# Six short GpSimd instructions in place of one long one: scaling the blocks of q tile by tile

## The chip, the cores and the metric

The kernel runs on one core of a Trainium2 chip. The metric is the device time of one execution in microseconds (us); lower is better. The engines of the core go by the profile's names: PE (TensorE matmul), PEld (TensorE weight load), DVE (VectorE), ACT (ScalarE), POOL (GpSimd), and SP (SyncE, which issues most DMAs). Each works through its own list of instructions in program order; semaphores tie the lists together.

## The reference

Windowed attention feeds a mixture of experts with one expert per token, and that feeds a two-layer network with a squared ReLU. Cut to what matters here:

```python
def _attn_ref(q, k, v):                      # q, k, v: (4, 8, 576, 64)
    scale = 1.0 / np.sqrt(D)                 # 0.125
    scores = scale * np.matmul(q, k.transpose(0, 1, 3, 2))
    ...                                      # heads 0-3: window 32; heads 4-7: window 32, dilation 4
    scores = np.where(masks[None, :, :, :], scores, -1000000000.0)
    scores = scores - np.max(scores, axis=-1, keepdims=True)
    attn = np.exp(scores)
    attn = attn / (np.sum(attn, axis=-1, keepdims=True) + 1e-09)
    return np.matmul(attn, v)

def _moe_ref(x, modality_id, w_gate, modality_bias, w1, w2):   # x: (2304, 512), 8 experts
    logits = x @ w_gate + modality_bias[modality_id]
    e_idx = np.argmax(logits, axis=1)
    ...                                      # gate_w: softmax weight of the chosen expert
    out[mask] = gate_w[mask, None] * (np.maximum(x[mask] @ w1[e], 0.0) @ w2[e])

def _moe2_ref(x, w_in, w_out):               # d_ff 2048
    h = np.maximum(x @ w_in, 0.0)
    return h * h @ w_out
```

## The kernel before, in words

**Attention.** There are 8 groups (4 batches, each with its plain and its dilated heads) of 6 tiles of 96 queries, so 48 units, handled one per round of a loop in `schedule`. For a unit, `A` writes the mask and the scores into a PSUM bank (the matmuls of L318 and L321, which read `q` and `kd`) and DVE takes the negated row maximum `nm` (L324). `C` is the exponential on ACT (`p`, L333). `D` transposes `p` on PE (L343) and copies it out on ACT (`pt`). `F` multiplies with `v` (L357) and DVE normalizes out of PSUM: `rs` (L360), its reciprocal `rc` (L363), the product `x` (L366). `H` transposes `x` on PE (L396), ACT copies the high part `xth` (L399), and DVE forms the low part `xtl` (L400) from the PSUM bank and `xth`. The steps of one round belong to different units: L396 in one round works on `x` of an earlier one, and it needs a bank from which `xtl` of the unit before has been read.

**Where q is scaled.** In the first round of a group, `A` calls `load` for the next group: SP issues the DMA of the whole block of q (128 partitions, 6 tiles, 2 x 96 columns, so 1152 numbers a partition) and of k, and GpSimd multiplies q by 0.125 in place (L299). The very first group is loaded in two halves; DVE scales the first half, GpSimd the second. So GpSimd has eight such instructions, one of 576 and seven of 1152 numbers a partition.

**What else DVE does.** One-time preparation (`setup`, up to L265) runs in round 3. Once a batch is through attention, `route` (L425 on, once a batch) and `select` (L529 on) work out which token goes to which expert. They are chains of very small DVE instructions on SBUF tiles; `schedule` deals them out between the attention steps of later rounds, a few at a time, in the fixed order of the program. So DVE's list alternates between attention steps, most of which read PSUM, and these small steps, most of which read and write SBUF only.

**Afterwards.** The experts' matmuls (class `Moe`) start between the last units and go on alone; the last stage (`Ffn`) decodes its weights with DVE, ACT and GpSimd (L864 to L880; `da` is the decoded tile, `raw` the loaded one), squares on GpSimd or DVE (`fsq`, L950), and multiplies (L940, L985). PE works through all of it in one fixed list.

Of the kernel before, what the change touches and what calls it, by code (L numbers as in the profile page):

```python
# [18 lines left out]
ALU = mybir.AluOpType  # L19
# [173 lines left out]
class Attention:  # L193
# [82 lines left out]
    def load(self, g, what):  # L276
        nc, ins = self.g.nc, self.g.ins
        if g >= 2 * B:
            return
        b, kind = divmod(g, 2)  # L280
        if "q" in what:
            self.qt[g] = self.qp.tile([128, NTL, 2, QT], F32, tag="q", name="q")
        if "v" in what:
            self.vt[g] = self.vp.tile([128, NTL, 260], F32, tag="v", name="v")
        plan = START if g == 0 else tuple((w, 0, NTL) for w in what)
        for w, t0, t1 in plan:
            if w == "i":
                nc.sync.dma_start(out=self.g.ident, in_=ins["c_ident"])
                continue
            if w == "m":  # L290
                nc.sync.dma_start(out=self.cmask, in_=ins["c_masks"])
                continue
            if w == "v":
                nc.sync.dma_start(out=self.vt[g][:, t0:t1], in_=ins["v"][b, kind, :, t0:t1])
                continue
            c0, c1 = t0 * QT, t1 * QT
            q = self.qt[g][:, t0:t1]
            nc.sync.dma_start(out=q, in_=ins["q"][b, kind, :, t0:t1])
            (nc.vector if g == 0 and t0 == 0 else nc.gpsimd).tensor_scalar(out=q, in0=q, scalar1=0.125, scalar2=None, op0=ALU.mult)  # L299
            for hb in range(2):  # L300
                nc.sync.dma_start(out=self.kd[g % 2][64 * hb:64 * hb + 64, :, hb, 32 + c0:32 + c1],
                                  in_=ins["k"][b, kind, 64 * hb:64 * hb + 64, :, c0:c1])
# [776 lines left out]
```

## Time and profile before

| | before |
|---|---|
| time, median of 3 runs (lowest, highest) | 828.16 us (826.91, 830.04) |
| the profiled execution: its time, its span | 828.4 us, 826.6 us |
| busy share of the span: PE, PEld | 96%, 82% |
| busy share of the span: DVE, ACT, POOL | 52%, 39%, 21% |
| mean granted clock of TensorE | 0.985 |

The span is the time from the first to the last instruction on the core; the 1.8 us between it and the time are outside the instructions. A busy share is a mean over stages with different limits, so POOL's 21% says nothing yet on whether one of its instructions holds somebody up. Rows of a timeline give the start, the duration, the engine, the line of the kernel, the operation, and the tile written and read; a bracket at the end is the idle time of that engine just ahead of the row, and what ended it. The granted clock is a share of TensorE's full speed.

### The profile page before, as it was taken

To read this page: it belongs to the slowest core of one execution; us is meant where nothing else is said; L and a number is where in the kernel's file an instruction comes from. 1 tells how busy PE (TensorE), PEld (TensorE's weight loads), DVE (VectorE), ACT (ScalarE), POOL (GpSimd) and SP (SyncE) were. 2 spreads that over 40 slices of the span, in tenths; PEclk is the share of its full clock that TensorE was granted. 3 is DMA by queue.
4 is the path that set the end of the run, shared out by engine and by line. 5 is a ranking of instruction groups with operands and counts; after the bars stand their busy time and mean duration, and the time that the engine had idled before them with its cause. 6 is when DMAs were issued, how large, how long until landed. Compare 5 with 4: busy or idle time off the path is not lost.

```text
span 826.6 us, 12554 instructions
## 1 busy us (share of the span) xinstructions
PE 790.4 (96%) x4273; PEld 675.3 (82%) x4273; DVE 428.9 (52%) x1124; ACT 325.2 (39%) x779; POOL 169.5 (21%) x197
## 2 busy tenths in 40 slices
PE   8999887899999999999898899999999999999996
PEld 5878776678888888888776789989989989998995
DVE  5787879743347777552399952242233234224222
ACT  3767656522244555552344532232232232223221
POOL 3135432014213333201155530010001001001001
PEclk9999988999999999999999999999999999999999
DMA  7666456020324444531245500010001001001000
GB/s 211 148 180 179 125 149 230 21 70 27 90 77 128 119 138 128 192 141 54 83 123 148 147 38 27 1 43 9 26 14 39 26 2 51 0 1 39 1 1 38
DMA packets 44810, 67.40 MB, mean 82 GB/s; under 512 B 6816, under 2 KB 28672, under 8 KB 44224
## 3 DMA queue, kind: packets, MB, share of 16 engines
q1 hardware_dynamic: 38720, 50.75, 21.2%
q0 software_dynamic: 3280, 10.76, 4.3%
q10 hardware_dynamic: 2736, 4.99, 1.6%
q8 instruction: 35, 0.57, 0.3%
q14 instruction: 39, 0.32, 0.1%
HBM read 129.65 MB, written 14.44 MB: 174 GB/s over the span
## 4 chain that ended last, share of the span: by engine, by line
issue 40%; DVE 5%; PE 2%; POOL 2%; DMA 1%; ACT 1%; POOLq 0%; ACTq 0%; DVEq 0%; SPq 0%
POOL out L990 1%; DMA raw<-in_wo 1%; DVE da L875 1%; PE bk L940 1%; DVE da L869 1%; DVE da L864 1%; DVE fhl L959 1%; PE bk L753 1%; DVE da L872 1%; PE bk L985 1%; POOL wol L880 0%; ACT dm L862 0%; ACT woh L879 0%; DVE yl L927 0%; DVE fout L989 0%
## 5 line engine op out<-in xcount | busy, mean ns | idle before, releaser
L950 DVE TENSOR_TENSOR fsq<-fr 128x384 f32<-128x384 f32 x84 | 46.9, 559 | 173.7 <-ACT fr L948 173.7
L940 PE MATMUL bk<-yh,wih 128*128 128x384 f32 x384 | 130.5, 340 | 3.3 <-ACTq L822 1.6
L940 PE MATMUL bk<-yl,wih 128*128 128x384 f32 x384 | 130.1, 339 | 1.3 <-DVE yl L927 1.3
L940 PE MATMUL bk<-yh,wil 128*128 128x384 f32 x384 | 129.9, 338 | 0.0
L948 ACT ACTIVATE fr<-bk 128x384 f32<-128x384 f32 x96 | 46.9, 488 | 188.0 <-PE bk L940 187.3
L985 PE MATMUL bk<-wol,fhh 128*128 128x512 f32 x288 | 113.5, 394 | 3.8 <-POOL wol L880 3.7
L985 PE MATMUL bk<-woh,fhh 128*128 128x512 f32 x288 | 115.0, 399 | 2.1 <-ACT woh L879 2.1
L985 PE MATMUL bk<-woh,fhl 128*128 128x512 f32 x288 | 113.3, 393 | 0.0
L990 POOL DMA_INDIRECT out<-fout,fidx x18 | 18.1, 1006 | 323.3 <-DVE fout L989 320.5
L940 PEld LDWEIGHTS bk<-yh,wih 128*128 128x128 f32 x384 | 72.5, 189 | 8.3 <-ACT yh L926 2.3
L959 DVE TENSOR_TENSOR fhl<-fsq,fhh 128x384 fp32r<-128x384 f32 x96 | 55.5, 578 | 45.0 <-ACT fhh L958 44.7
L940 PEld LDWEIGHTS bk<-yl,wih 128*128 128x128 f32 x384 | 72.4, 189 | 5.8 <-DVE yl L927 2.6
L940 PEld LDWEIGHTS bk<-yh,wil 128*128 128x128 f32 x384 | 72.6, 189 | 0.0
L958 ACT ACTIVATE fhh<-fsq 128x384 fp32r<-128x384 f32 x96 | 50.3, 524 | 50.2 <-DVE fsq L950 48.7
L985 PEld LDWEIGHTS bk<-wol,fhh 128*128 128x128 f32 x288 | 54.2, 188 | 14.4 <-POOL wol L880 6.0
L985 PEld LDWEIGHTS bk<-woh,fhl 128*128 128x128 f32 x288 | 54.2, 188 | 13.1 <-DVE fhl L959 0.4
L723 PE MATMUL bk<-w1h,xh 128*128 128x512 f32 x152 | 63.4, 417 | 0.8 <-DVE htl L739 0.8
L985 PEld LDWEIGHTS bk<-woh,fhh 128*128 128x128 f32 x288 | 54.2, 188 | 11.7 <-ACT woh L879 3.8
L333 ACT ACTIVATE p<-bk,nm 96x128 f32<-96x128 f32 x192 | 53.9, 363 | 19.6 <-DVE nm L324 11.1
L753 PE MATMUL bk<-w2h,hth 128*128 128x512 f32 x152 | 61.0, 401 | 0.0
L723 PE MATMUL bk<-w1l,xh 128*128 128x512 f32 x152 | 60.9, 400 | 0.0
L723 PE MATMUL bk<-w1h,xl 128*128 128x512 f32 x152 | 60.8, 400 | 0.0
(173 smaller groups left out, 1399.8 us busy)
## 6 DMA issues: line engine op xcount, KB each, us to landing
st<-in_w SPq DMA_DIRECT2D x41, 2048.0 KB
raw<-in_wi SPq DMA_DIRECT2D x32, 256.0 KB
raw<-in_wo SPq DMA_DIRECT2D x32, 256.0 KB
v<-in_v SPq DMA_DIRECT2D x7, 780.0 KB
q<-in_q SPq DMA_DIRECT2D x7, 576.0 KB
kd<-in_k SPq DMA_DIRECT2D x14, 288.0 KB
xd<-x SPq DMA_DIRECT2D x40, 96.0 KB
yb<-y ACTq DMA_DIRECT2D x13, 256.5 KB
```

The source lines that it names most:

```text
L333: self.g.nc.scalar.activation(out=p[:, h, :], in_=ps[:, h, :], func=AF.Exp, bias=nm[:, h:h + 1], scale=1.0)
L723: nc.tensor.matmul(ps, a[:, c, :], w[:, c, sl], start=k == 0, stop=k == 11)
L753: nc.tensor.matmul(ps, a[:, c, :], w[:, c, :], start=k == 0, stop=k == 23)
L864: nc.vector.tensor_scalar(out=a, in0=raws[new][:, :, 1], scalar1=3, scalar2=0x3FFFFFF8, op0=ALU.logical_shift_left, op1=ALU.bitwise_and)
L869: nc.vector.scalar_tensor_tensor(out=a, in0=raws.pop(old)[:, :, 0], scalar=29, in1=a, op0=ALU.logical_shift_right, op1=ALU.bitwise_or)
L940: nc.tensor.matmul(ps, w[:, c, f * 128:(f + 1) * 128], a[:, c, :], start=k == 0, stop=k == 11)
L948: nc.scalar.activation(out=r, in_=ps, func=AF.Relu)
L950: (nc.gpsimd if blk == 0 and f > 3 else nc.vector).tensor_tensor(out=s, in0=r, in1=r, op=ALU.mult)
L958: nc.scalar.activation(out=hh, in_=s, func=AF.Copy)
L959: nc.vector.tensor_tensor(out=hl, in0=s, in1=hh.bitcast(F32), op=ALU.subtract)
L985: nc.tensor.matmul(acc[t], a[:, sl], w[:, f, :], start=f == 0 and j == 0, stop=f == NF - 1 and j == 2)
L990: dma = nc.gpsimd.indirect_dma_start(out=out, out_offset=bass.IndirectOffsetOnAxis(ap=self.idx[:, i:i + 1].bitcast(U32), axis=0), in_=o, i ...
```

## The change

Where GpSimd scales a block of q, the loop now issues one instruction per tile of 192 numbers a partition: three for the second half of the first group and six for each of the other seven groups, 45 in place of 8. What DVE scales, the DMAs and all tiles stay as they are. The lines behind the edit move down by five (L321 is L326 and so on).

```diff
             q = self.qt[g][:, t0:t1]
             nc.sync.dma_start(out=q, in_=ins["q"][b, kind, :, t0:t1])
-            (nc.vector if g == 0 and t0 == 0 else nc.gpsimd).tensor_scalar(out=q, in0=q, scalar1=0.125, scalar2=None, op0=ALU.mult)
+            if g == 0 and t0 == 0:
+                nc.vector.tensor_scalar(out=q, in0=q, scalar1=0.125, scalar2=None, op0=ALU.mult)
+            else:
+                for t in range(t0, t1):
+                    q = self.qt[g][:, t]
+                    nc.gpsimd.tensor_scalar(out=q, in0=q, scalar1=0.125, scalar2=None, op0=ALU.mult)
             for hb in range(2):
```

On GpSimd's list, the start of the program before (the half block, the first whole block, three small fills of `setup`, the next block; the brackets are the semaphores that a row waits for, DMAHW those of DMAs):

```order
L299 ISA
L299 TENSOR_SCALAR q<-q 128x576 [waits DMAHW6_49,Pool_49]
L299 TENSOR_SCALAR q<-q 128x1152 [waits DMAHW0_49]
L247 MEMSET reset 96x48
L248 MEMSET reset 96x8 [waits Pool_49]
L249 MEMSET tbl 128x144
L299 TENSOR_SCALAR q<-q 128x1152 [waits DMAHW7_49,DVE_49,PE_49]
```

The same place now:

```order
L304 ISA
L304 TENSOR_SCALAR q<-q 128x192 [waits DMAHW6_49,Pool_49]
L304 TENSOR_SCALAR q<-q 128x192 x2
L304 TENSOR_SCALAR q<-q 128x192 [waits DMAHW0_49]
L304 TENSOR_SCALAR q<-q 128x192 x5
L247 MEMSET reset 96x48
L248 MEMSET reset 96x8 [waits Pool_49]
L249 MEMSET tbl 128x144
L304 TENSOR_SCALAR q<-q 128x192 [waits DMAHW7_49,DVE_49,PE_49]
```

Each long row has become one short row that waits for the DMA, and two or five more that wait for nothing; what stands around them is in the same order as before.

On PE's list, one round of attention in the second group before:

```order
L357 MATMUL bk_70<-v,pt 96x65 x4
L318 LDWEIGHTS mask
L318 MATMUL bk_67<-mask 96x512
L321 MATMUL bk_67<-kd_140,q 96x256 x2
L396 MATMUL bk_73<-ident,x 128x96 [waits DVE_49]
L396 MATMUL bk_73<-ident,x 128x96
```

The same round now:

```order
L362 MATMUL bk_70<-v,pt 96x65 x4
L323 LDWEIGHTS mask
L323 MATMUL bk_67<-mask 96x512
L326 MATMUL bk_67<-kd_140,q 96x256 [waits Pool_49]
L326 MATMUL bk_67<-kd_140,q 96x256
L401 MATMUL bk_73<-ident,x 128x96 [waits DVE_49]
L401 MATMUL bk_73<-ident,x 128x96
```

Every unit's scores now wait for the scaling of their own tile, where only the first unit of a block waited before; no row has changed its place. DVE's, ACT's and SP's lists hold the same rows in the same order.

## Rows read from the trace of the kernel before

**Rows 1.** Timeline, 28.5 to 34 us: a block of q beside attention alone.

```profile
29.11 3.13 POOL L299 TENSOR_SCALAR q<-q 128x1152 f32<-128x1152 f32 x1 [10.42 <-DVE rs L360]
...
30.52 0.34 DVE L400 TENSOR_TENSOR xtl<-bk,xth 128x192 fp32r<-128x192 f32 x1
```

**Rows 2.** Timeline, 14.5 to 20 us: the first place.

```profile
15.17 3.13 POOL L299 TENSOR_SCALAR q<-q 128x1152 f32<-128x1152 f32 x1 [3.48 <-DMA q<-in_q]
15.21 3.06 DVE L265 TENSOR_TENSOR bias<-bias,btmp 96x192 f32<-96x192 f32 x1
...
18.19 0.15 DVE L360 TENSOR_SCALAR rs<-bk 96x4 f32<-96x4 f32 x1
...
19.05 0.39 PE L396 MATMUL bk<-ident,x 96*128 96x96 f32 x2 [2.07 <-DVE x L366]
```

**Rows 3.** Timelines, 57.5 to 66 us: the second place, all engines, then DVE.

```profile
58.12 3.18 POOL L299 TENSOR_SCALAR q<-q 128x1152 f32<-128x1152 f32 x1 [9.51 <-DMA q<-in_q]
...
58.39 2.93 DVE L486 COPY carry<-rcum 96x8 f32<-96x8 f32 x1
...
61.52 0.38 PE L396 MATMUL bk<-ident,x 96*128 96x96 f32 x2 [1.88 <-DVE xtl L400]
...
63.59 0.35 DVE L400 TENSOR_TENSOR xtl<-bk,xth 128x192 fp32r<-128x192 f32 x1
```

**Rows 4.** Timeline, 90 to 96 us: the third place.

```profile
90.64 2.96 DVE L483 TENSOR_TENSOR_SCAN rcum<-reset,rtin 96x48 f32<-96x48 f32 x1
...
94.23 0.39 PE L396 MATMUL bk<-ident,x 96*128 96x96 f32 x2 [2.08 <-DVE xtl L400]
```

**Rows 5.** Timeline, 109.5 to 124 us: the fourth place.

```profile
110.21 3.03 DVE L542 TENSOR_SCALAR scj<-sci 1x8 int32<-1x8 int32 x1
...
115.49 0.58 PE L396 MATMUL bk<-ident,x 96*128 96x96 f32 x2 [2.30 <-DVE xtl L400]
```

**Rows 6.** Windows, PE alone: length, busy (instructions), granted clock, DMA share, GB/s.

```profile
61.50:65.50 4.00, 3.96 (x36) 1.00 0.42 67
94.00:99.00 5.00, 4.77 (x30) 0.66 0.43 101
115.00:122.50 7.50, 7.01 (x33) 0.54 0.62 163
```

**Rows 7.** Groups of POOL instructions by shape.

```profile
L299 POOL TENSOR_SCALAR q<-q 128x1152 f32<-128x1152 f32 x7 | 21.9, 3135 | 56.8 <-DMA q<-in_q 21.0 <-PE bk L357 13.3 <-PE bk L343 12.2
...
L299 POOL TENSOR_SCALAR q<-q 128x576 f32<-128x576 f32 x1 | 1.7, 1677 | 6.8 <-DMA q<-in_q 6.8
```

**Rows 8.** Timeline, 415 to 434 us: two POOL instructions back to back, and DVE.

```profile
418.68 0.74 POOL L880 TENSOR_TENSOR wol<-da,woh 128x256 fp32r<-128x256 f32 x1 [1.20 <-ACT woh L879]
418.71 0.99 DVE L875 SCALAR_TENSOR_TENSOR da<-dm,da 128x256 f32<-128x256 f32 x1
419.38 1.01 POOL L950 TENSOR_TENSOR fsq<-fr 128x384 f32<-128x384 f32 x1
419.62 0.91 DVE L864 TENSOR_SCALAR da<-raw 128x256 int32<-128x256 int32 x1
```

**Rows 9.** Timeline of PE, 0 to 60 us: the mask matmuls of three units.

```profile
15.74 0.38 PE L318 MATMUL bk<-mask 96*96 96x512 bf16 x1
...
26.39 0.38 PE L318 MATMUL bk<-mask 96*96 96x512 bf16 x1
...
28.62 0.38 PE L318 MATMUL bk<-mask 96*96 96x512 bf16 x1
```

**Rows 10.** Waits of PE: engine, line, for whom; us in total, times, longest.

```profile
PE bk L321 <- POOL q L299: 0.2, 1, 0.2
```

**Rows 11.** Timeline, 248 to 252 us: three POOL and DVE rows of the decoding.

```profile
249.16 0.99 POOL L702 DMA_INDIRECT gx<-xd,sc  x1 [0.51 <-POOL sc L701]
...
249.75 1.47 DVE L872 SCALAR_TENSOR_TENSOR da<-raw,da 128x256 int32<-128x256 int32 x1
250.18 0.75 POOL L880 TENSOR_TENSOR wil<-da,wih 128x256 fp32r<-128x256 f32 x1
```

## The prediction

> **What bounds the kernel now.** I first looked at where the edited line lies: all blocks of q are scaled in the first 114 us, in the attention stage. There I read the timeline of all engines around each of the eight GpSimd instructions, to see which other engine changes its pace while one runs. In four of them nobody does. The block from 29.11 to 32.24 [rows 1] is typical: DVE's `xtl`, which reads one PSUM and one SBUF tile, takes its ordinary 0.34 us in the middle of it, and a round of attention lasts 2.23 us (two mask matmuls in a row start at 26.39 and 28.62, [rows 9]), just as without a block. So the busy time of GpSimd itself is not on the path.
>
> In the other four DVE stands still until the GpSimd instruction is over. At 15.21 the last instruction of `setup`, a sum of two SBUF tiles, takes 3.06 us and ends at 18.27, when the scaling ends at 18.30 [rows 2]. At 58.39 a copy of 8 numbers a partition takes 2.93 us and ends at 61.32, the scaling at 61.30 [rows 3]. The scan at 90.64 takes 2.96 us [rows 4], a shift of 8 integers on one partition at 110.21 takes 3.03 us [rows 5]. All four read and write SBUF only. The sizes of these instructions have nothing to do with their times; the end of the GpSimd instruction has.
>
> That reaches the path, since DVE's list mixes these small steps with attention steps. Behind each of them stands an `x` or an `xtl`, and PE's L396 waits for it: 2.07, 1.88, 2.08 and 2.30 us of idle PE [rows 2 to 5], 8.3 us together. There is a second loss: in the five microseconds from 94 us PE has a mean granted clock of 0.66, in the 7.5 from 115 us of 0.54, that is mostly the lower of its levels (1.2 in place of 2.4 GHz), while behind the idle of 1.88 us the clock stayed at 1.00 [rows 6]. In these two windows PE is busy nearly all the time, so its pace sets the rounds.
>
> **The change part by part.** *The short instruction.* The two sizes that ran, 576 and 1152 numbers, took 1677 and 3135 ns [rows 7]: 2.53 ns a number and 0.22 us fixed. One of 192 numbers should take 0.71 us, six of them 4.2 us, so GpSimd works 1.1 us longer for a block, 8 us in all. Nobody waits for that by itself: in the first whole block tile 0 is scaled at 15.9 us and first used after 18 us, and a further tile is wanted only each 2.23 us. PE's 37 added waits find their tile done; I cost them at nothing. If each cost what the separate wait instructions of GpSimd's queue last at most, below 0.05 us, that would be under 2 us, but the other waits on PE's list are of this kind and show no such gap.
>
> *The half block.* PE waited 0.2 us for it [rows 10]. Its first tile is now done a microsecond earlier. k may land no earlier than that, so I take a gain of 0.2, between 0 and 0.3.
>
> *What DVE waits now.* What the trace must tell is whether DVE gets its turn between two GpSimd instructions that stand back to back. In the decoding there is such a pair [rows 8]: L880 ends at 419.42, L950 has begun at 419.38. DVE's L875, which reads two SBUF tiles and started at 418.71, ends at 419.70, well inside L950, which runs to 420.39: it got in at the border. The next DVE instruction, L864, started at 419.62 and then had to wait nearly to the end of L950 (420.53). So they take turns: each GpSimd instruction holds up at most one DVE instruction of this kind, for a little less than its own length. The page SBUF — State Buffer of the Trainium skill (section Who interferes with whom) names the cause: DVE and GpSimd share one port pair under an exclusive lock for a whole instruction, so the loser blocks fully. The first two places bear this out to 0.03 us.
>
> *The first place.* Only one SBUF-only instruction is left in DVE's list there. It gets in at about 15.8 in place of 17.9 us, and the attention steps behind it read PSUM and run freely. PE then has no idle time: its wait for `x` began at 16.98 (19.05 less 2.07), and `x`, which followed 0.86 us behind the start of `rs` at 18.19, is now there by 16.8. From the mask matmul at 15.74 to the one at 26.39 are 10.65 us for three rounds, where three of 2.23 us are 6.7 [rows 9]: 3.9 us lost, idle time, lower clock and late ACT together. I take back 3.7, between 2.1 (idle PE alone) and 3.9.
>
> *The second place.* Here six SBUF-only steps of `route` (L486, L489, L491, L493, L499, L502) follow one another, with `xtl`, `rs`, `rc` and `x` in between. Each meets another of the six short instructions. The copy ended 0.02 us behind the scaling [rows 3] though it needs some 0.17 us itself, so an instruction of 0.71 holds DVE for about 0.55. Going through the list with that, I get waits of about 0.3, 0.55, 0.3, 0.5, 0.25 and 0.4 us: 2.3 us in place of nearly all of 2.93. DVE would reach the second `xtl`, now at 63.59 [rows 3], perhaps 0.1 us earlier. Gain 0.1; the bounds are -1.0 and +1.9 (all of the idle PE).
>
> *The third place.* The same chain from the scan on gives 2.6 us of waits, so DVE gains nearly nothing. But PE's 2.08 us of idle time are split in two of about a microsecond, since the first `xtl` comes early and the second late. Each is shorter than the 1.88 us behind which the clock stayed up, so I expect the full clock: 4.77 us of busy time at 0.66 are 3.15 us at 1.00 [rows 6], a gain of 1.6. Bounds: 0 (clock falls all the same) and 3.7 (with the idle time).
>
> *The fourth place.* In `select` all small steps are SBUF-only, but with attention steps between them; I get waits of 0.45, 0.4, 0.35, 0.1 and 0.5 us, and `nm` and `xtl` 0.7 us earlier. PE's idle time falls from 2.30 to 1.6 us. If the clock stays up, 7.01 us at 0.54 shrink to 3.8 [rows 6], but DVE's chain has to run as well, so of these 3.2 us I count 1.0. Gain 1.7, between 0.7 and 5.5 (2.30 and 3.2).
>
> *The sum*: 0.2 + 3.7 + 0.1 + 1.6 + 1.7 = 7.3 us. What follows is one fixed order on PE, whose loads and weights are issued by the same lists, so I let all of it pass to the end. The profiled execution took 828.4 us, 0.2 over the median of the runs shown: 828.4 - 7.3 = 821.1, say **821.0 us**.
>
> **The rivals.** *(A) The lock isn't given up between the six.* Then DVE waits through the whole block: 4.0 us (six of 0.71, with the small overlaps that back-to-back instructions show) in place of 3.13, in four places, +3.6 us: **832.0**. It decides if DVE misses the first border. For it: DVE's L872 at 249.75 took 1.47 us, past the end of L702 at 250.15 and nearly to that of L880 at 250.93 [rows 11]. Against it: rows 8, where both are element-wise work as here. The GPSIMD Engine Reference of the Trainium skill (section 2.1, Instruction dispatch) says that a core of GpSimd starts the next instruction as soon as its own share is done; by that rule neighbours could overlap and leave no border. In rows 8 the trace doesn't agree; rows 11 would fit.
>
> *(B) Turns cost as much as the long wait.* In the last three places the chains are dense, and PE's clock falls as before: 0.2 + 3.7 + 0.1 + 0 + 0.7 = 4.7, **823.7**. For it: the six waits in a row. Against it: shorter single idles of PE.
>
> *(C) DVE wins most borders.* If GpSimd is slow to come back behind a DVE instruction, several small steps pass at once, and the idle and the low clock go everywhere: 0.2 + 3.9 + 1.9 + 3.7 + 5.5 = 15.2, **813.5**. Against it: L864 in rows 8 was too late after one turn.
>
> *(D) The gain is given back* where experts start or weights land: **828**, no change. For it, loads have times of their own; against it, they are issued behind the steps that move.
>
> **How the numbers follow.** The forecast 0.52, (A) 0.08, (B) 0.20, (C) 0.12, (D) 0.08. Less than 0.5% (4.1 us, about what a measurement of this kernel can tell from no change; from 828.16 down to 824.0) is same. Faster: forecast, (C) and half of (B), 0.74. Same: half of (B) and (D), 0.18. Slower: (A), 0.08. The range 816 to 827 leaves out (A), most of (D) and half of (C), 0.2 in all; the likeliest case's own range is 818.5 to 823.5.
>
> **What would show it.** Each step right: L304 x45 with a mean near 0.70 us; the sum of L270 (L265 before) below 0.9 us and PE without idle at that L401; DVE instructions in the other three places that last 0.3 to 0.7 us several in a row, where one lasted 3; the clock near 1.00 in what are now 94 to 99 and 115 to 122 us. Wrong: a DVE instruction of 4 us (A), the same rounds with a low clock (B), or mask matmuls 7 us earlier at 120 us and not at 400 (D).

## The result, and the profile after

| | before | after |
|---|---|---|
| time, median (lowest to highest; runs) | 827.53 us (826.43 to 830.04; 4) | 815.75 us (812.57 to 816.65; 4) |
| the profiled execution: time, span | 828.4, 826.6 us | 815.87, 814.1 us |
| ratio, 95% interval | | 0.9837 [0.9809, 0.9866] |

The kernel is 11.8 us faster; the forecast was 7.3, and the time lies a quarter of a microsecond below the range. Behind the edit each line has moved by five, so L299 is L304, L396 is L401, L486 is L491.

Where the time came from is read from mask matmuls, one a unit, by how much earlier each starts than the same one in the kernel before. The one at 15.74 us before starts 0.8 earlier, that at 26.39 4.1, at 68.51 6.5, at 102.61 10.3, at 135.35 14.3, and the span is 12.5 shorter. The differences are the gains of the four places: 3.3, 2.3, 3.8 and 4.0 us, 13.5 together; 0.8 came ahead of them and 1.8 was lost behind.

The groups of POOL instructions, first row:

```profile
L304 POOL TENSOR_SCALAR q<-q 128x192 f32<-128x192 f32 x45 | 30.0, 694 | 53.0 <-PE bk L348 14.6 <-PE bk L326 13.6 <-PE bk L401 12.4
```

A short instruction takes 0.69 us, where a whole block took 3.14 [rows 7]. The timeline at the four places, the blocks and DVE's longest lines beside them, and at the end two rows that a later experiment is about:

```profile
14.43 0.35 DVE L265 TENSOR_TENSOR bias<-bias,btmp 96x192 f32<-96x192 f32 x1
...
14.92 3.96 POOL L304 TENSOR_SCALAR q<-q 128x192 f32<-128x192 f32 x6 [2.97 <-DMA q<-in_q]
...
53.32 4.09 POOL L304 TENSOR_SCALAR q<-q 128x192 f32<-128x192 f32 x6 [8.98 <-PE bk L326]
...
54.27 0.17 DVE L491 COPY carry<-rcum 96x8 f32<-96x8 f32 x1
...
54.74 0.37 DVE L496 TENSOR_TENSOR rpo<-rpo,rwit 96x48 f32<-96x48 f32 x1
...
84.46 0.28 DVE L491 COPY carry<-rcum 96x8 f32<-96x8 f32 x1
...
86.16 0.31 DVE L507 TENSOR_SCALAR rci<-rpos 96x6 int32<-96x6 int32 x1
...
100.09 0.32 DVE L547 TENSOR_SCALAR scj<-sci 1x8 int32<-1x8 int32 x1
...
102.35 0.33 DVE L567 TENSOR_TENSOR ssel<-sge 1x12 f32<-1x12 f32 x1
...
120.93 1.80 DVE L514 CAST rrf<-rri 96x6 f32<-96x6 int32 x1
...
122.92 2.18 DVE L520 TENSOR_SCALAR rhot<-iota,rrf 96x128 f16<-96x128 f32 x1
```

Beside the blocks nobody is held for long. The copy, the scan and the shift that took 2.93, 2.96 and 3.03 us [rows 3 to 5] take 0.17, 0.24 and 0.32, and no small step beside a block lasts more than 0.18 us longer than alone. Two steps have passed before their block begins: the scan at the third place, and at the first place the sum L265 (the prediction's L270; it stands ahead of the edit and keeps its number). PE's waits for k up to 125 us, then three rows of PE with a wait ahead of them, then four windows of PE (columns as in rows 6):

```profile
PE bk L326 <- DMA kd<-in_k: 1.3, 2, 0.9
```

```profile
17.97 1.08 PE L326 MATMUL bk<-kd,q 128*96 128x256 f32 x4 [0.39 <-DMA kd<-in_k]
...
105.37 0.32 PE L422 MATMUL bk<-xtl,wg 128*16 128x288 f32 x1 [0.84 <-DVE xtl L405]
...
123.05 0.39 PE L401 MATMUL bk<-ident,x 96*128 96x96 f32 x2 [0.75 <-DVE xtl L405]
```

```profile
89.50:94.00 4.50, 4.50 (x38) 1.00 0.48 174
...
105.50:112.50 7.00, 6.46 (x52) 1.00 0.57 164
126.00:130.00 4.00, 3.19 (x13) 0.52 0.09 25
...
146.00:150.00 4.00, 3.51 (x9) 0.58 0.06 15
```

Of the 8.3 us of idle PE ahead of the transposes [rows 2 to 5] nothing is left, and the clock is 1.00 where it was 0.66 and 0.54 [rows 6]. The wait at 123.05 is another one, which the kernel before had too:

```profile
137.34 0.39 PE L396 MATMUL bk<-ident,x 96*128 96x96 f32 x2 [0.74 <-DVE xtl L400]
```

New are the waits of 0.4 us for k at the first place and of 0.8 us for `xtl` at the fourth.

### The profile page after: what moved, and what is told of

It reads as the page before. It is cut to its first block, busy times and chain, and to the rows that moved or that the text cites. A ratio compares the mean times of both kernels' runs of the same rounds, so it can differ in the third digit from the quotient of the medians.

```text
span 814.1 us, 12599 instructions
## 1 busy us (share of the span) xinstructions
PE 784.6 (96%) x4273; PEld 671.7 (83%) x4273; DVE 418.9 (51%) x1124; ACT 325.1 (40%) x779; POOL 173.9 (21%) x234
## 4 chain that ended last, share of the span: by engine, by line
issue 40%; DVE 5%; PE 2%; DMA 2%; POOL 1%; ACT 1%; POOLq 0%; ACTq 0%; DVEq 0%; SPq 0%
DMA raw<-in_wo 2%; POOL out L995 1%; DVE da L880 1%; PE bk L945 1%; DVE fhl L964 1%; DVE da L874 1%; DVE da L869 1%; PE bk L758 1%; DVE da L877 1%; PE bk L990 1%; ACT dm L867 0%; ACT woh L884 0%; DVE fsq L955 0%; DVE yl L932 0%; DVE fout L994 0%
## 5 line engine op out<-in xcount | busy, mean ns | idle before, releaser
L758 PE MATMUL bk<-w2h,htl 128*128 128x512 f32 x152 | 59.5, 391 | 0.0
```

The lines of the kernel that those rows point to most:

```text
L758: nc.tensor.matmul(ps, a[:, c, :], w[:, c, :], start=k == 0, stop=k == 23)
```

## The experiments

How much each kernel's mask matmuls gain on the kernel before, in us, from one of those five to the next, as above; "w1l" is from the one at 135.35 to the last, at 146.78, and "rest" from there to the end of the span. Each row is one profiled execution.

| kernel | start | 1st | 2nd | 3rd | 4th | w1l | rest |
|---|---|---|---|---|---|---|---|
| after | 0.8 | 3.3 | 2.3 | 3.8 | 4.0 | -0.5 | -1.2 |
| after, second profile (e9_after) | 0.7 | 3.2 | 2.2 | 3.6 | 4.5 | 0.8 | 0.2 |
| e1_two | -0.5 | 3.1 | 1.6 | 3.2 | 3.9 | 0.6 | 0.2 |
| e2_three | -1.7 | 3.9 | 1.9 | 3.3 | 3.6 | 0.0 | -1.4 |
| e3_twelve | 0.5 | 2.5 | 2.3 | 3.8 | 4.1 | 0.7 | 0.4 |
| e5_three | 0.2 | 1.6 | 2.2 | 3.6 | 4.3 | 0.1 | 0.2 |
| e8_1088 | 0.4 | 3.3 | 1.1 | 3.1 | 3.8 | 0.2 | 0.0 |
| e6_w1l | 0.5 | 2.1 | 2.1 | 3.9 | 4.3 | 4.2 | -1.3 |
| e7_dec | 0.8 | 3.3 | 2.4 | 3.7 | 4.3 | 4.2 | 0.1 |
| e10_best | 0.7 | 2.6 | 2.1 | 3.7 | 4.4 | 4.1 | -0.2 |

Three theories stood at the outset. **T**, that of the forecast: a GpSimd instruction holds DVE from its start to just before its end, and DVE gets one turn between two. **S**: the hold begins only some 0.3 us after the start, so that short instructions hardly hold. **L**: nothing about the pieces but where they happen to lie makes the difference.

**The hold by itself (p1_hold).** A kernel that leaves out the whole computation: GpSimd scales 2304 numbers in pieces of one size, while DVE runs 90 small copies that have nothing to do with it.

```python
for i in range(TOT // n):
    nc.gpsimd.tensor_scalar(out=q[:, i*n:(i+1)*n], in0=q[:, i*n:(i+1)*n], scalar1=0.125, scalar2=None, op0=ALU.mult)
for i in range(M):
    nc.vector.tensor_copy(b[:, 8*i:8*i+8], a[:, 8*i:8*i+8])
```

> A kernel that only measures: GpSimd multiplies 2304 numbers a partition in pieces of 2304, 1152, 576, 384, 288, 192 and 96, back to back, while DVE issues 90 copies (then 90 sums of two tiles) of 8 numbers from SBUF to SBUF; at the end the same with PSUM as DVE's source, and with GpSimd subtracting two tiles in pieces of 256 and 128. It leaves out the whole of the attention, the experts and the network, so its time is of no use beside the other kernels. Theory S (a GpSimd instruction holds DVE only from some 0.3 to 0.4 us after its start on, so short ones hardly hold it): one long DVE instruction for each piece, of about the piece's length less 0.5 us: 5.4 us at 2304, 2.6 at 1152, 1.2 at 576, 0.7 at 384, 0.2 at 192, none at 96; and several short DVE instructions between two long ones, whatever the size. Theory T (turns, as in the forecast: held from the start of a piece to just before its end): one long one for each piece, of its length less 0.15 us (0.55 at 192, 0.3 at 96), and one short DVE instruction, seldom two, between them. Theory L (the attention stage was lucky in how its steps fell): as T here. All: with PSUM as the source no DVE instruction is held.

One line's instructions in a window (count, then shortest, median and longest in ns): DVE's copies while GpSimd works, with one piece of 2304, four of 576, and twelve of 192:

```profile
L45 DVE COPY b<-a x11: 167/300/6018, 34.1 to 40.2; 128x8 f32<-128x8 f32 x11
...
L45 DVE COPY b<-a x62: 157/270/643, 58.6 to 65.2; 128x8 f32<-128x8 f32 x62
...
L45 DVE COPY b<-a x86: 157/192/333, 85.4 to 93.7; 128x8 f32<-128x8 f32 x86
```

The 2304 let nobody in. With 576 there is no hold of 1.5 us (T), nor one of 1.1 (S): none lasts much over half a microsecond, and 62 copies pass. Undisturbed copies end 0.073 us apart, so a hold is a wider gap between two ends. Read so, **each piece of 576 holds twice: for 0.56 us from 0.13 us after its start, and for 0.56 us up to its end. Between the two 0.43 us are free**, in which half a dozen copies pass. The same two holds are seen at 384 (0.39 and 0.40 us, 0.29 free), 288 (0.32 and 0.30, 0.22) and 192 (0.24 and 0.22, 0.14). Where DVE's instruction is a sum of two SBUF tiles, only the first hold is there (0.55 at 576); copies out of PSUM are held at neither of the two sizes tried (1152 and 192). The two holds do not act alike. In the second the copies beside 576 go on starting 0.073 us apart, and the eight that have started end within 0.08 us just behind it: it delays whoever waits for a result, and costs DVE's pace next to nothing. (Beside 1088, whose second hold is longer, eight start as well, and then none until it ends.) T and S fell. The new theory, **R**: up to some size a piece holds DVE at its beginning and its end only, above it throughout.

The page SBUF — State Buffer of the Trainium skill (Who interferes with whom) has an exclusive lock that is kept for the whole instruction; from 1152 numbers on the rows agree, below they don't. It also says that a DVE instruction with two SBUF inputs contends only with what GpSimd reads. By that the first hold would be GpSimd's reading and the last its writing, which fits the sums; no run here shows what GpSimd does in between.

**Other sizes of piece (e1, e2, e3).** In place of six of 192:

```diff
-for t in range(t0, t1):                 # 192 each
-    q = self.qt[g][:, t]
+for t in range(t0, t1, 3):              # e1: two of 576; e2: step 2, three of 384
+    q = self.qt[g][:, t:t + 3]          # e3: self.qt[g][:, t, h] for h in 0, 1: twelve of 96
```

> Blocks of q in two pieces of 576 numbers (1.68 us each) in place of six of 192. Theory S: a piece holds a DVE step for up to 1.2 us and then leaves a gap of some 0.4 us in which two or three small steps pass; the four places cost about half of what they did in the kernel before, and TensorE idles too briefly for its clock to fall: 818 to 821 us. Theory T: a chain of small steps loses 1.5 us to each piece, 3 us in all, as before: 822 to 827. Theory L: anything from 814 to 826, depending on which step meets which piece.

> Blocks of q in three pieces of 384 numbers (1.19 us each). Theory S: a piece holds a step for up to 0.7 us: 815.5 to 818 us, single DVE steps of up to 0.9 us in the three chains. Theory T: three turns of 1.0 us each, 820 to 825. Theory L: no order among two, three, six and twelve pieces.

> Blocks of q in twelve pieces of 96 numbers (some 0.46 us each, 5.5 us a block, 1.5 us more than with six). Theory S: nothing is held any more, but six pieces had left only some 0.5 us of waits in a place: 814 to 816.5 us, DVE steps in the chains at their ordinary 0.15 to 0.25 us. Theory T: twelve turns of 0.3 us, more than the chain has steps for: waits of 0.2 to 0.3 us at nearly each step, 817 to 821. Theory L: within 814 to 820.

Measured against 828.03 us of the kernel before: two pieces 816.15, ratio 0.985 [0.9832, 0.9868]; three 817.13, 0.9854 [0.9832, 0.9876]; twelve 813.79, 0.9835 [0.98, 0.987]. One cut in the middle brings most of what five bring, where S gave 818 to 821 us and T 822 to 827. Three pieces are no faster than two; in the profiled execution their start was 1.7 us late, and the times of the two kernels overlap. The timeline of e1 at the first two places has the holds of half a microsecond:

```profile
15.71 0.70 DVE L265 TENSOR_TENSOR bias<-bias,btmp 96x192 f32<-96x192 f32 x1
...
56.27 0.53 DVE L496 TENSOR_TENSOR rpo<-rpo,rwit 96x48 f32<-96x48 f32 x1
...
57.78 0.59 DVE L507 TENSOR_SCALAR rci<-rpos 96x6 int32<-96x6 int32 x1
```

Here L265 did meet its block (15.36 us), as before, and lost 0.35 us in place of 2.7.

**Where the hold becomes whole (p2_size).** The same kind of kernel, with two pieces of each size from 576 to 1152, then other instructions on DVE and two-input subtractions on GpSimd.

> The kernel only measures and leaves out all of the reference's work: two GpSimd scalings of n numbers a partition in a row (576 to 1152), beside 110 small DVE copies; then scans, shifts of integers, and sums of an SBUF and a PSUM tile beside 1152, 576 or 192 numbers; then GpSimd subtractions of 1024, 512 and 128 numbers. Theory R (GpSimd holds DVE only while it reads its numbers and while it writes them, with a free stretch between, as long as the piece is no longer than some size between 576 and 1152; a longer piece holds from start to end): up to that size two holds of about a third of the piece each (0.56 us at 576, 0.7 at 704, if still below), from the next size on one hold as long as the piece (over 2 us). Scan and shift: one hold of about 2.9 us at 1152, holds of 0.56 at 576 and of 0.23 at 192. Subtractions: 1024 holds for about 2.2 of its 2.36 us, 128 for 0.34 of 0.42. The sums that read PSUM are not held. Theory T (a piece holds DVE for its whole length less about 0.15 us, and DVE gets one turn between two): holds of n x 2.53 ns less 0.15 at every size, 1.6 at 704, 0.55 at 192, with one DVE instruction in between.

DVE's copies beside two pieces of 1088 and two of 1152, then the sums of an SBUF and a PSUM tile beside 1152:

```profile
L50 DVE COPY b<-a x40: 158/164/1235, 95.4 to 100.7; 128x8 f32<-128x8 f32 x40
...
L50 DVE COPY b<-a x13: 158/213/3127, 106.9 to 113.2; 128x8 f32<-128x8 f32 x13
...
L58 DVE TENSOR_TENSOR b<-a,acc x88: 156/186/209, 228.7 to 235.0; 128x8 f32<-128x8 f32 x88
```

R holds, and the limit is sharp: **1088 numbers hold for 0.98 us, leave 0.73 free, and hold 1.15; 1152 hold for 3.0 us without a break.** The blocks of q lie 64 numbers above the limit. Scans (two SBUF inputs) lose 2.77 us at 1152, 0.55 once at 576, 0.27 once at 192; shifts of integers on one partition behave like copies. Subtractions are different: with two inputs a piece of 128 holds 0.34 of 0.41 us, one of 256 (in the first kernel) 0.61 of 0.69, one of 1024 2.25 of 2.4, in one hold each.

**1088 and 64 (e8_1088).** The sharpest form of the question in the kernel itself:

```diff
-for t in range(t0, t1):
-    q = self.qt[g][:, t]
+whole = self.qt[g][:, t0:t1].rearrange("p t r c -> p (t r c)")
+for a, z in ([(0, 1088), (1088, n)] if w == 6 else [(0, n)]):    # w: tiles, n: numbers
+    q = whole[:, a:z]
```

> Each block of 1152 numbers in a piece of 1088 and one of 64, for every kv head: hardly shorter than the one long instruction. Theory R with the size read from the second measuring kernel (1088 numbers hold DVE for 0.98 us at the start and 1.15 us at the end and leave 0.73 us free between, 1152 hold it for 3.0 us without a break): the sum at the first place, or any single step, waits at most 1.2 us in place of 2.9, chains wait about 2 of 3 us; 40 to 75% of the change's gain, 818 to 823 us. Theory T (a hold as long as the piece): a wait of 2.7 us in each place, 825 to 829.

817.67 us, ratio 0.9885 [0.984, 0.9929], against 814.0 for the change and 827.58 for the kernel before on the same chip: 9.9 of 13.6 us. That is 73% of the gain, where R gave 40 to 75% (its 818 us is missed by 0.3, on the fast side) and T had 825 us and more. An instruction shortened by 64 of its 1152 numbers does most of what six do. Its timeline at the second place, block and small steps:

```profile
54.55 3.30 POOL L307 TENSOR_SCALAR q<-q 128x1088 f32<-128x1088 f32 x2 [11.30 <-DMA q<-in_q]
...
54.70 0.97 DVE L494 COPY carry<-rcum 96x8 f32<-96x8 f32 x1
55.59 0.19 DVE L497 TENSOR_TENSOR rpo<-rcum,rtot 96x48 f32<-96x48 f32 x1
...
55.97 0.19 DVE L499 TENSOR_TENSOR rpo<-rpo,rwit 96x48 f32<-96x48 f32 x1
56.19 0.25 DVE L501 TENSOR_TENSOR rpo<-rpo,roh 96x48 f32<-96x48 f32 x1
...
56.75 0.79 DVE L507 CAST rpos<-rposf 96x6 int32<-96x6 f32 x1
```

The same copy that took 2.93 us [rows 3] is let go after 0.97, four small steps pass at their own pace, and the cast at 56.75 meets the second hold, to 57.54, when the 1088 are done. The row of POOL holds the piece of 64 too; e8's lines stand three further down than those of the change.

**Only three blocks in pieces (e5_three).** The blocks of groups 4, 6 and 7 are those of the second, third and fourth place.

```diff
-for t in range(t0, t1):
-    q = self.qt[g][:, t]
+n = 1 if g in (4, 6, 7) else t1 - t0
+for t in range(t0, t1, n):
+    q = self.qt[g][:, t:t + n]
```

> Six instructions only for the three later blocks that met DVE's small steps (the blocks of kv heads 4, 6 and 7), one long instruction for all others, the first place among them. Theory R: the other blocks meet nobody, so only the first place's gain is lost, 3.3 us less a part where the program's start happens to be early: 818 to 820 us against 815.75 for the change. Theory L (the first place's gain came from an earlier start of the program and not from the pieces): 815.5 to 816.5. If other blocks matter too: above 820.

817.86 us, ratio 0.9904 [0.987, 0.9937]: 0.1 below R's 818 and 1.4 above L's 816.5, which by itself does not decide. Its lines stand one further down than those of the change. Its timeline at the first place, and the wait there:

```profile
14.66 3.33 POOL L305 TENSOR_SCALAR q<-q 128x1152 f32<-128x1152 f32 x1 [3.13 <-DMA q<-in_q]
...
15.05 2.92 DVE L265 TENSOR_TENSOR bias<-bias,btmp 96x192 f32<-96x192 f32 x1
```

```profile
PE bk L402 <- DVE x L372: 1.9, 1, 1.9
```

The sum met its long block as before and was held as before. In e1, e2 and e8 it met its block too, in pieces, and lost 0.35, 0.25 and 0.8 us (1.16 for the sum in e8); there the place gained 3.1, 3.9 and 3.3 us. So the pieces count and L falls as an account of all the gain. In the change itself, though, the sum passed ahead of its block, so the 3.3 us of that execution were not earned by the pieces of this block. The sum passed ahead in all six executions whose half block was in pieces of 192 or 96 (after, e9, e3, e6, e7, e10; start 0.5 to 0.8 us early) and met its block in all others (before, e1, e2, e5, e8; start between 1.7 late and 0.4 early). e5 still gains 1.6 us at the place, since the clock behind the idle stayed up. Windows of PE from 20 to 24 us, of the kernel before and then of e5:

```profile
20.00:24.00 4.00, 4.00 (x24) 0.60 0.39 83
```

```profile
20.00:24.00 4.00, 4.00 (x33) 1.00 0.40 76
```

Four microseconds at 0.60 are 2.4 at 1.00: the 1.6. So the clock behind one idle of 2 us is not the same in every execution, and a place's worth moves by as much. The other three places keep their gains, and the four blocks that met nobody [rows 1] cost nothing in one piece.

**The next long hold (e6_w1l, e7_dec).** What still holds DVE in the changed kernel is GpSimd's w1l (the low part of an expert's weights, L687), two subtractions of 1024 numbers from 120.3 us on; beside them two of DVE's small steps last 1.80 and 2.18 us (the last rows of the timeline after). e6 cuts each in eight. e7 also cuts the 64 subtractions of the decoding (256 numbers) in half.

```diff
-eng.tensor_tensor(out=lo[:, k, :], in0=src[:, k, :], in1=hi[:, k, :].bitcast(F32), op=ALU.subtract)
+w = 128 if eng is nc.gpsimd else src.shape[2]                  # e6
+for c0 in range(0, src.shape[2], w):
+    s = slice(c0, c0 + w)
+    eng.tensor_tensor(out=lo[:, k, s], in0=src[:, k, s], in1=hi[:, k, s].bitcast(F32), op=ALU.subtract)
...
-nc.gpsimd.tensor_tensor(out=lo, in0=v, in1=hi.bitcast(F32), op=ALU.subtract)
+w = hi.shape[2] // 2                                           # e7
+for s in (slice(0, w), slice(w, 2 * w)):
+    nc.gpsimd.tensor_tensor(out=lo[:, :, s], in0=v[:, :, s], in1=hi[:, :, s].bitcast(F32), op=ALU.subtract)
```

> The change, and besides it GpSimd's two w1l subtractions of 1024 numbers in eight pieces of 128 each. Theory R: a piece of 128 with two inputs holds DVE for 0.34 of 0.42 us, so the two DVE steps that now last 1.80 and 2.18 us last at most 0.6; PE's 4.3 us of waits for x there shrink to about 1, and the stretches of low clock behind them (126 to 133 and 146 to 150 us) go or shrink: 3 to 5 us, 811 to 813. Rival W: the pieces take GpSimd 6.8 in place of 4.7 us, and the tables that it makes next come later: 815 to 818.

> e6, and besides it each of the 64 subtractions of 256 numbers on GpSimd in the decoding in two halves of 128. Theory R: two halves hold DVE for 0.34 us each, where one of 256 held it for 0.61, so nothing is won: the time of e6 within 1.5 us, or up to 4 us more, since GpSimd itself works 0.15 us longer for each. Theory T: more turns let DVE, which is busy nearly all the time there, get in twice as often: 2 to 6 us less than e6.

e6 took 811.51 us, ratio 0.9825 [0.9784, 0.9866], e7 811.03, 0.983 [0.979, 0.987], against 827.0 for the kernel before on the same chip. The timeline of e6 has the two steps so:

```profile
122.36 0.31 DVE L514 CAST rrf<-rri 96x6 f32<-96x6 int32 x1
...
122.86 0.29 DVE L520 TENSOR_SCALAR rhot<-iota,rrf 96x128 f16<-96x128 f32 x1
```

In the table this stretch gains 4.2 us, where the change had -0.5 and 0.8. PE's waits for `x` ahead of L362 from 110 to 150 us fall from 4.3 to 2.8 (the longest from 3.0 to 1.4), not to the 1 that was expected, and from 126 to 130 us the clock is 1.00 where it was 0.52. In e6 it fell later, to 0.71 from 142 to 146 us, in e7 and e10 it did not. The halves in the decoding are worth nothing: from 147 us to the end e7 gains 0.1 us. That is against T and as R has it, for which the time held counts and not the number of turns. But the same would come out if DVE's holds there were not on the path at all; no run tells these two apart.

**The best version beside the change (e9_after, e10_best).** Both once more, with six runs each; e10 is e7.

> The changed kernel once more, for a comparison with the next one on the same chip: 813 to 817 us by every theory.

> The change with the two w1l subtractions in eight pieces and the decoding's subtractions in halves once more. Theory R: 809 to 812.5 us, 3 to 5 below the change alone, since the waits behind w1l are gone and the clock stays up behind them. Rival W (the difference was that of single runs): within 1.5 us of the change alone.

The change 814.0 us, ratio 0.9843 [0.9809, 0.9878]; with w1l and the decoding in pieces 810.81 us, 0.9799 [0.9766, 0.9832]. The intervals just overlap, but the slowest of e10's six runs (812.43) lies below the fastest of e9's (812.86), e6 and e7 stood at 811.5 and 811.0 too, and the stretch that the gain comes from is in the table three times.

## Why the prediction was wrong

**What bounds the kernel** was read rightly: GpSimd's own time, 6.4 us longer (30.0 us for the 45 rows against 21.9 and 1.7 [rows 7], where the forecast had 8), costs nothing, and nearly all of the gain comes from the four places.

**The step that failed is the size of the hold.** The prediction let "an instruction of 0.71" hold DVE "for about 0.55" and added six of those to 2.3 us and 2.6 us a chain. The figure came from the end of a long hold [rows 3] and from a pair of two-input instructions [rows 8]. Both are true of what they show: 1152 numbers hold throughout, and 256 with two inputs for 0.61 of 0.69 us. Neither is true of 192 numbers with one input, which hold for 0.24 and 0.22 us with a gap in between, and a sum or a scan only for the first. The delays in the rows after are 0.03 to 0.18 us a step, no more than about 0.7 us in a place.

**The four places.** First: 3.7 forecast, 3.3 measured. The sum was right: 2.07 us of idle PE and 1.6 of low clock from 20 to 24 us are gone, and PE waits 0.39 us for k instead, which the sum did not have. In all seven executions that show this wait (0.4 us in the change, 1.7 in e6) it and the gain in the table add up to 3.7. The profile names k's DMA for it in three of them and a GpSimd instruction in the others; since the scaling of the tile needed was long done, I take it for k's in all. Second: 0.1 forecast, 2.3 measured, above its bound of 1.9: the round with the wait of 1.88 us was 2.1 us longer than now, and the next one 0.2. Third: 1.6 and 3.8; fourth: 1.7 and 4.0. In both the clock stayed up as forecast, but the idle times went as well, where the prediction left PE 2.1 us in two pieces, and 1.6. All in all 8.3 us of idle are gone, and the three low stretches give 1.6 (first place), 1.6 and 3.2 us by the prediction's own conversion [rows 6]. Less the two new waits of 0.4 and 0.8 us that is 13.5, as measured; place by place this sum is off by up to 0.7.

**The half block.** PE's wait for it is gone; in its place it waits 0.9 us for k's DMA. The start was 0.8 us earlier, where the forecast had 0.2. It was 0.5 to 0.8 earlier in all executions with the half block in pieces of 192 or 96, and between 1.7 later and 0.4 earlier in the others. That points to the pieces, but the DMAs at the start vary as well, and no run separates the two.

**What was lost behind** (1.8 us) is not a cost that the change always has: the second profile of the same kernel gained 1.0 in the same stretches. In the first, the clock is 0.58 from 146 to 150 us, in the second 1.00.

**The rivals.** (C) came nearest with 813.5 (its own sum gives 813.2) and had three of the four places nearly right, but not the reason. GpSimd is not slow to come back: its next piece starts 0.02 us before the last has ended, and the first hold begins 0.13 us after that start. What lets DVE's chains through is the short hold, at whose end they go on within the same piece. (A) is excluded by p1: between back-to-back pieces of 192 or 576 copies do pass. (B) took the forecast's hold and falls with it. Of (D) nothing is left once the two profiles of the change are compared.

## What to carry to other kernels

Before a hold seen beside one instruction is carried over to a shorter one, measure it at both sizes and for the same kind of operands; here cutting 64 of 1152 numbers off did most of the work. Where small DVE steps on SBUF lie in the chain that feeds PE, look for GpSimd instructions above the limit (1088 numbers of one fp32 input were below it, 1152 above) and for two-input ones of any length, and cut those that meet such steps. Cutting two-input instructions shortens the single wait but not the time held, which paid beside w1l and not in the decoding.

## What the runs showed of the hardware

Beside a GpSimd scaling of one fp32 tile the hold is not one thing: two holds with a free stretch between them up to 1088 numbers a partition (0.56, 0.43 and 0.56 us at 576), and an unbroken one from 1152 (3.0 us). This was read from one execution of each measuring kernel, and no size between the two was run. Copies and integer shifts meet both, sums and scans of two SBUF tiles only the first, and what reads PSUM (88 sums beside 1152 numbers, the longest 209 ns) neither. The granted clock behind an idle PE of 2 us differed between executions: 0.60 from 20 to 24 us in the kernel before, 1.00 in e5 behind an idle of 1.9.
